# Masking the strided heads of four batches by a multiplication on VectorE, and spreading the first expert's weights

## The chip, the cores and the metric

The kernel runs on one core of one Trainium2 chip. The metric is the device time of one execution in microseconds. A core has five engines with queues of their own: TensorE (PE, with its weight loads shown apart as PEld), VectorE (DVE), ScalarE (ACT), GpSimd (POOL) and SyncE (SP, which here only issues transfers).

## The reference

Two blocks follow each other: sparse attention, then a mixture of experts with one expert for each token.

```python
# attention: batch 8, heads 8, S = 576, head size 64
rel = pos[:, None] - pos[None, :]
mask_local = (rel >= 0) & (rel < 32)
mask_strided = (rel >= 0) & (pos[None, :] % 32 == pos[:, None] % 32)
masks = mask_local for heads 0 to 3, mask_strided for heads 4 to 7
scores = np.where(masks, q @ k.T / np.sqrt(D), -1e9)
attn = softmax(scores);  x = attn @ v          # heads side by side: 576 x 512 for each batch
# experts: 8 experts, 512 -> 1024 -> 512
logits = x @ w_gate;  local_gate = sigmoid(x @ w_local)
e = argmax(logits) if s == 0 or local_gate < 0.5 else the previous token's e
out = p[e] * (relu(x @ w1[e]) @ w2[e])         # p: softmax of the logits
```

A masked score contributes nothing to the numerator and nothing to the sum. Setting it far below zero ahead of the exponential, or multiplying its exponential by zero, gives the same sum.

## The kernel before

The kernel has two stages: attention with the router (function `attention`, up to about 165 us), then the experts (`Experts.run`, to the end). The change is in the first.

**Steps.** Attention runs over 32 pairs of heads, batch by batch: pairs 0 and 1 of a batch are local, 2 and 3 strided. Each pair is two units (`Unit`, g = 0 and 1). The loop at L433 is software-pipelined by hand (the scheduler is off, so each engine's queue has the order of the program text). Step n issues, in this order: the load of q and k of pair n + 4 (L436); a piece of the first expert's weights in steps 5 to 12 (L438); scores and mask of the two units of pair n (L442, L443); the store of x of a pair finished two steps ago (L445); the transposes of pair n - 2 (`turn_x`, L447); values and norm of pair n - 1 (L450, L451); up to two of the weights' sums (L457); for finished batches the gates (L463), the store of probabilities and the logits (L467); and router work of the list `also` (L472). So step 4b + 2 carries the gates of batch b - 1, and step 4b + 1 its logits.

**A strided pair.** The 576 positions are split into 32 residue classes of 18. Four blocks hold 7 classes (126 positions) and one holds 4 (72). Within a block, two positions of different classes must not see each other. Unit 0 covers two blocks, unit 1 two and the small one. `scores` makes the score block keys by queries with the two heads on separate halves of TensorE's rows (L261), ScalarE takes the exponential out of PSUM (L265), `values` multiplies by v with a column of ones (L285), and `norm` divides by the sum on VectorE (reciprocal L298, product L299).

**The masks before.** A local unit's exponentials are multiplied by 0 or 1 on VectorE (L272). A strided unit gets its mask ahead of the scores: TensorE multiplies an identity in bf16 by `maskS` (0 or -8e9) into the PSUM bank, two matmuls for each unit (L255), and the scores accumulate on top.

**Logits and gates.** `logits` (L348) multiplies the transposed x by the router's weights into the one bank of `psT`; ScalarE and VectorE copy it out in turn (L351, L352, L354, L357), and the exponentials of the next step stand behind these copies in ScalarE's queue. `turn_x` uses the same bank. `gates` (L367 on TensorE, then twelve small operations L372 to L392 on VectorE and one on ScalarE) takes a buffer of `psV`, which has two: it must wait until `norm` has read it.

**The first expert's weights.** `Weights.load` brings them in eight pieces of 512 KB through SP's queue (w1 in four, L706, then w2 in four, L709). The experts multiply matrices of two by two blocks with seven products in place of eight, for which sums of weight blocks are needed: 16 operations of 128x512 on VectorE (`Weights.sums`, L714), made from step 10 on, two in a step. Router work of the first four batches begins at step 19: transposes of the codes (19), a scan (L547, step 20), counts (L550 to L554, step 21), slots (22), their way back (23), and a table from 24 on (`where` L609 to L614, `what` L620, `some` L627).

**Loads.** Buffers for q and k are five (`inp`), so a load waits on SP until a step's scores are done. From batch 2 on SP also issues the stores of x (L311, L317; twelve for each batch).

Of the kernel before, what the change touches and what calls it, by code (L numbers as in the profile page):

```python
# [8 lines left out]
F32 = mybir.dt.float32  # L9
# [3 lines left out]
Alu = mybir.AluOpType  # L13
# [6 lines left out]
B, H, S, DH = 8, 8, 576, 64  # L20
# [19 lines left out]
GK, GL = PL * GC, PL * GR  # L40
# [18 lines left out]
WARM = 10  # L59

FILL = 4

ARMS = 7
SKIP = 8192
# [18 lines left out]
def across(ap, shape):  # L83

    return ap.rearrange("a (o b) -> a o b", o=1).to_broadcast(shape)
# [60 lines left out]
def attention(ctx, tc, qkl, qks, vl, vs, wg, xd, ident, router, moe):  # L146

    nc = tc.nc
    sums, probs, codes = router.sums, router.probs, router.codes
    consts = ctx.enter_context(tc.tile_pool(name="consts", bufs=1))  # L150
# [28 lines left out]
    def busy(n):  # L179
        for _ in range(n):  # L180
            ps = psV.tile([P, 512], F32, name="vps")
            nc.tensor.matmul(ps, lhsT=warm[:, 0:P], rhs=warm, start=True, stop=True)  # L182
# [23 lines left out]
    maskS = consts.tile([GK, 2 * GK + GL], BF16, name="maskS")  # L206
# [3 lines left out]
    for n, c in blocks:  # L210

        i, div = consts.tile([GK, 1], I32, name=f"row{n}"), consts.tile([GK, 1], F32, name=f"div{n}")
# [7 lines left out]
    n = GK  # L220
    nc.vector.tensor_copy(maskS[:, 0:2 * n].rearrange("p (a x) -> p a x", a=2), across(apart[n], [n, 2, n]))
    nc.vector.tensor_copy(maskS[:, 2 * n:], apart[GL])
    fold = consts.tile([P, E + 1], F32, name="fold")
    ci = consts.tile([P, E], I32, name="ci")
    down = consts.tile([P, E], F32, name="down")
    pi = consts.tile([P, CH], I32, name="pi")
    pos8 = consts.tile([P, CH], F32, name="pos8")
    start = consts.tile([P, CH], F32, name="start")

    def more_constants():  # L230

        nc.vector.tensor_reduce(fold, ident.rearrange("p (k x) -> p x k", k=DK)[:, 0:E + 1], axis=AX.X, op=Alu.add)


        nc.gpsimd.iota(ci, pattern=[[-1, E]], base=E, channel_multiplier=0)
        nc.vector.tensor_copy(down, ci)
        nc.gpsimd.iota(pi, pattern=[[E * P, CH]], base=E, channel_multiplier=E)
        nc.vector.tensor_copy(pos8, pi)
        nc.vector.tensor_scalar(start, pos8, float(E), None, Alu.is_equal)

    def spans(u):

        if u.local:
            return [(3 * u.g + i, LQ, i * LQ) for i in range(3)]
        return [(j, GK if j < GT - 1 else GL, i * GK) for i, j in enumerate(range(2 * u.g, 2 + 3 * u.g))]

    def scores(u):
        t = st["qk", u.b, u.pair]
        kb, width = (LK, LQ) if u.local else (GK, GK)
        ps = psS.tile([P, 2, 512], F32, name="sps")  # L250
        sp = spans(u)
        n = sp[-1][2] + sp[-1][1]
        if not u.local:
            for h in range(2):
                nc.tensor.matmul(ps[0:GK, h, 0:n], lhsT=identb[0:GK, 0:GK],  # L255
                                 rhs=maskS[:, 0:n], start=True, stop=False, skip_group_check=True)
        for j, w, c in sp:
            m = kb if u.local else w
            for h in range(2):
                r = slice(h * DH, (h + 1) * DH)  # L260
                nc.tensor.matmul(ps[0:m, h, c:c + w], lhsT=t[r, S + j * width:S + j * width + m],  # L261
                                 rhs=t[r, j * width:j * width + w],
                                 start=(u.local and c == 0), stop=True, skip_group_check=True)
        e = work.tile([P, 2, 2 * GK + GL], F32, name="e")
        nc.scalar.activation(e[0:kb, :, 0:n], ps[0:kb, :, 0:n], Act.Exp, bias=0.0, scale=1.0 / DH ** 0.5)  # L265
        u.e = e

    def mask(u):
        if u.local:
            ev = u.e[:, :, 0:3 * LQ]  # L270
            m = maskL[:, 3 * u.g:3 * u.g + 3].rearrange("p a x -> p (a x)")
            nc.vector.tensor_tensor(ev, ev, m.rearrange("p (o x) -> p o x", o=1).to_broadcast([LK, 2, 3 * LQ]),  # L272
                                    op=Alu.mult)

    def values(u):
# [26 lines left out]
    def store_x(u):  # L302

        q = nc.gpsimd if u.b < 2 else nc.sync
        src = st["x", u.b, u.local]
        dst = xd[u.b * S:(u.b + 1) * S, (0 if u.local else D // 2):(D // 2 if u.local else D)]
        for a in range(2):
            if u.local:
                w = LQ // 2
                o = dst.rearrange("(t a p) d -> a p t d", a=2, p=w)[a]  # L310
                q.dma_start(out=o, in_=src[a * (P - w):a * (P - w) + w])  # L311
                continue
            for j in range(GT):
                c = GC if j < GT - 1 else GR
                w = c * PL // 2
                o = dst.rearrange("(p c) d -> p c d", c=STRIDE)[a * PL // 2:(a + 1) * PL // 2, j * GC:j * GC + c]
                q.dma_start(out=o, in_=src[a * (P - w):a * (P - w) + w, j])  # L317

    def turn_x(b, pair):
        if pair == 0:  # L320
            st["xT", b] = rows.tile([P, DK, S], F32, name="xT")
        local = pair < PAIRS // 2
        src = st["x", b, local][:, :, (pair % 2) * P:(pair % 2 + 1) * P]
        ps = psT.tile([P, 8, P], F32, name="tps")
        n = LT if local else GT
        for t in range(n):
            nc.tensor.transpose(ps[:, t], src[:, t], ident)  # L327
        o = st["xT", b][:, pair]

        def halves(o, i, w):  # L330
            nc.scalar.copy(out=o.rearrange("p (t a x) -> p t a x", a=2, x=w // 2),
                           in_=pick_halves(i, w))

        if local:
            halves(o, ps[:, 0:LT], LQ)
        else:
            halves(o[:, 0:4 * GK], ps[:, 0:GT - 1], GK)
            halves(o[:, 4 * GK:], ps[:, GT - 1:GT], GL)
# [55 lines left out]
    def store_p(b):  # L394
        dst = xd[b * S:(b + 1) * S, D:DX]
        full = S // P
        nc.gpsimd.dma_start(out=dst[0:full * P].rearrange("(t p) c -> p t c", p=P), in_=probs[:, 0:full, b])
        nc.gpsimd.dma_start(out=dst[full * P:], in_=probs[0:S - full * P, full, b])
# [14 lines left out]
        u.n = n  # L413

    also = {n: [] for n in range(len(units) + 3)}
    also[1] = [more_constants]
    also[2] = [router.constants]
    n = PAIRS * RB + 3
# [4 lines left out]
    m = n  # L423
    rooms = (moe.spot[0].rearrange("p a x -> p (a x)")[:, 0:1024], moe.spot[1].rearrange("p a k x -> p (a k x)"),
             moe.spot[2].rearrange("p i a x -> p (i a x)"))
    early = router.table(0, bank, rooms)
# [5 lines left out]
    steps = []  # L432
    for n in range(len(units) + 3):  # L433
        if n < len(units):
            if n + ahead < len(order):
                load(*order[n + ahead])  # L436
            if 5 <= n < 13:
                moe.W[0].load(nc, moe.w1, moe.w2, 0, n - 5)  # L438
            if n == 10:
                steps = moe.W[0].sums(nc.vector)  # L440
            for u in units[n]:
                scores(u)  # L442
                mask(u)  # L443
        if 0 <= n - 2 < len(units) and order[n - 2][1] % 2 == 1:
            store_x(units[n - 2][1])  # L445
        if 0 <= n - 2 < len(units) and n != len(units):
            turn_x(*order[n - 2])  # L447
        if 0 <= n - 1 < len(units):
            for u in units[n - 1]:
                values(u)  # L450
                norm(u)  # L451
        if n == len(units):
            turn_x(*order[n - 2])
            moe.turn(moe.first, spare, 0)
        elif n == len(units) + 1:
            busy(FILL)
        for do in steps[:2]:  # L457
            do()
            steps.remove(do)
        for b in range(B):  # L460
            last = PAIRS * b + PAIRS - 1
            if n == last + 3:
                gates(b)  # L463
            if n == last + 4 and b < B - 1:
                store_p(b)
            if n == last + 2:
                logits(b)  # L467
        if n == len(units) + 1:
            moe.turn(moe.first, bank, 1)
            busy(2)  # L470
            moe.row_sums(moe.first)
        for do in also[n]:  # L472
            do()
# [1056 lines left out]
```

## Time and profile before

| | us |
|---|---|
| median of three runs | 689.92 (687.54 to 690.97) |
| the profiled execution, whole | 686.27 |
| its span, first to last instruction | 684.5 |
| TensorE busy in the span | 666.4 |
| VectorE busy in the span | 356.7 |
| ScalarE busy in the span | 198.2 |
| mask matmuls L255, 64 of them, first and last start | 10.4 and 153.2 |
| multiplications L272, 32 of them, mean of one | 0.753 |

Durations below are from the one profiled execution. In lines of the timeline the columns are start, duration, engine, line, operation, output and input with shapes, count, and in brackets the idle time of the engine before and what ended it. In the chain of waits they are start, duration, engine, output tile and line. A TensorE matmul's end is modelled and neighbours overlap, so the chain's pieces, not the mean durations, say what a group of matmuls takes. Most fp32 matmuls appear as two records.

### The profile page before, as it was taken

How to read it: one execution, taken by the hardware profiler on the slowest of the kernel's cores; microseconds unless marked ns; L12 is line 12 of the kernel's file. 1: busy time of each engine (PE TensorE's matmuls, PEld its weight loads, DVE VectorE, ACT ScalarE, POOL GpSimd, SP SyncE). 2: the span in 40 equal slices, each digit the busy share in tenths (PEclk: the TensorE clock that was granted, in tenths of full speed). 3: DMA queues.
4: the chain of work that ended last, by engine and by line, in shares of the span. 5: the costliest groups of instructions: out<-in, count | busy, mean ns of one | idle time of the engine just before them, and what ended most of it. 6: DMA issues, size and time to landing. Idle time of an engine off the chain costs nothing.

```text
span 684.5 us, 14864 instructions
## 1 busy us (share of the span) xinstructions
PE 666.4 (97%) x6055; PEld 574.2 (84%) x6056; DVE 356.7 (52%) x821; ACT 198.2 (29%) x365; POOL 117.7 (17%) x144
## 2 busy tenths in 40 slices
PE   9999999999999999999999999999999999999994
PEld 6888887887998999589989999997799899699493
DVE  6558866865895437126532654651256546522131
ACT  3454453544312221222222122122222132221220
POOL 3440000012021113111111202202111113121001
PEclk9999999999999999999999999999999999999998
DMA  9999878733611172171236118111612622021001
GB/s 322 402 377 329 274 250 279 255 114 121 226 36 43 50 268 76 40 275 40 57 120 204 56 29 294 51 32 40 251 48 65 234 75 72 34 57 41 18 9 35
DMA packets 35800, 95.80 MB, mean 140 GB/s; under 512 B 4790, under 2 KB 11702, under 8 KB 35628
## 3 DMA queue, kind: packets, MB, share of 16 engines
q1 hardware_dynamic: 27164, 71.41, 29.6%
q0 software_dynamic: 7936, 22.38, 10.1%
q8 instruction: 66, 1.08, 0.6%
q14 instruction: 106, 0.87, 0.4%
q10 hardware_dynamic: 528, 0.07, 0.1%
HBM read 74.66 MB, written 19.69 MB: 138 GB/s over the span
## 4 chain that ended last, share of the span: by engine, by line
PE 93%; DVE 3%; issue 1%; ACT 1%; DMA 1%; POOL 0%; SPq 0%; DVEq 0%; POOLq 0%
PE lps L817 30%; PE mps L853 28%; PE sps L261 6%; PE vps L285 5%; PE lps L908 4%; PE mps L919 4%; PE tps L327 3%; PE xps L760 2%; PE mps L949 2%; PE lps L929 2%; PE sps L255 2%; PE vps L367 1%; PE tps L348 1%; DVE xl L299 1%; PE vps L182 1%
## 5 line engine op out<-in xcount | busy, mean ns | idle before, releaser
L773 POOL DMA_INDIRECT out_dram<-y,tab x40 | 46.1, 1153 | 351.4 <-DVE y L805 247.4
L817 PE MATMUL lps<-tt,ws 128*128 128x128 f32 x768 | 91.8, 275 | 0.3 <-issue 0.3
L817 PEld LDWEIGHTS lps<-tt,ws 128*128 128x128 f32 x768 | 88.6, 192 | 0.6 <-issue 0.5
L853 PE MATMUL mps<-wt,k 128*128 128x256 f32 x384 | 85.7, 380 | 0.0
L853 PEld LDWEIGHTS mps<-wt,k 128*128 128x128 f32 x384 | 72.8, 190 | 9.9
L817 PE MATMUL lps<-xt,w1t 128*128 128x128 f32 x512 | 63.2, 276 | 3.0 <-ACT y L955 1.9
L817 PEld LDWEIGHTS lps<-xt,w1t 128*128 128x128 f32 x512 | 60.4, 192 | 6.5 <-ACT y L955 3.7
L805 DVE TENSOR_TENSOR h<-lps,u 128x512 f32<-128x512 f32 x48 | 33.2, 691 | 58.3 <-PE lps L817 58.2
L853 PE MATMUL mps<-w2t,h 128*128 128x256 f32 x256 | 60.5, 379 | 0.0
L747 POOL DMA_INDIRECT x<-xd,gi x40 | 41.1, 1027 | 84.8 <-issue 34.7
L265 ACT ACTIVATE e<-sps 128x576 f32<-128x576 f32 (+1 forms) x64 | 41.3, 650 | 40.0 <-PE sps L261 39.2
L853 PEld LDWEIGHTS mps<-w2t,h 128*128 128x128 f32 x256 | 47.4, 190 | 5.8
L261 PE MATMUL sps<-qk 64*128 64x96 f32 (+2 forms) x704 | 51.2, 283 | 0.1
L804 ACT ACTIVATE h<-h 128x512 f32<-128x512 f32 x48 | 30.3, 630 | 70.1 <-DVE h L805 69.0
L261 PEld LDWEIGHTS sps<-qk 64*128 64x128 f32 (+2 forms) x704 | 43.1, 185 | 8.5 <-issue 7.2
L804 ACT ACTIVATE h<-lps 128x512 f32<-128x512 f32 (+1 forms) x28 | 15.7, 563 | 81.8 <-PE lps L817 65.6
L805 DVE TENSOR_TENSOR u<-lps,p 128x512 f32<-128x512 f32 x16 | 11.1, 691 | 52.5 <-PE lps L817 31.6
L753 ACT ACTIVATE x<-x 128x512 f32<-128x512 f32 (+1 forms) x40 | 27.1, 717 | 34.5 <-DMA x<-xd,gi 21.1
L761 ACT COPY xt<-xps 128x512 f32<-128x512 f32 (+1 forms) x38 | 20.3, 565 | 49.3 <-PE xps L760 49.3
L817 PE MATMUL lps<-xt,ws 128*128 128x128 f32 x256 | 31.3, 275 | 0.0
L817 PE MATMUL lps<-tt,w1t 128*128 128x128 f32 x256 | 31.3, 275 | 0.0
L853 PE MATMUL mps<-w2t,k 128*128 128x256 f32 x128 | 30.4, 380 | 0.0
(236 smaller groups left out, 974.5 us busy)
## 6 DMA issues: line engine op xcount, KB each, us to landing
w1t<-in_w_dram SPq DMA_DIRECT2D x7, 2048.0 KB
w2t<-in_w_dram SPq DMA_DIRECT2D x7, 2048.0 KB
qk<-in_qkl_dram SPq DMA_DIRECT2D x16, 592.0 KB
qk<-in_qks_dram SPq DMA_DIRECT2D x16, 576.0 KB
vl<-in_vf_dram SPq DMA_DIRECT2D x8, 780.0 KB
vs<-in_vg_dram SPq DMA_DIRECT2D x8, 639.8 KB
xd<-xl SPq DMA_DIRECT2D x12, 288.0 KB
xd<-xs SPq DMA_DIRECT2D x48, 63.0 KB
```

Source lines behind the costliest of these rows:

```text
L261: nc.tensor.matmul(ps[0:m, h, c:c + w], lhsT=t[r, S + j * width:S + j * width + m], rhs=t[r, j * width:j * width + w], start=(u.local and ...
L265: nc.scalar.activation(e[0:kb, :, 0:n], ps[0:kb, :, 0:n], Act.Exp, bias=0.0, scale=1.0 / DH ** 0.5)
L285: nc.tensor.matmul(ps[a * HALF:(a + 1) * HALF, h, i], lhsT=u.e[0:m, h, q0:q0 + HALF], rhs=vt[0:m, j, 2 * i2 + h], start=(i == 0 and h == 0 ...
L747: self.nc.gpsimd.indirect_dma_start(out=r.x[0:r.m, i], out_offset=None, in_=self.xd[0:r.rows], in_offset=bass.IndirectOffsetOnAxis(ap=r.gi ...
L753: self.nc.scalar.activation(r.x[0:r.m, i, 0:D], r.x[0:r.m, i, 0:D], Act.Copy, scale=r.gate[i][0:r.m])
L773: s = self.nc.gpsimd.indirect_dma_start(out=self.out, out_offset=bass.IndirectOffsetOnAxis(ap=r.si[i][0:r.m], axis=0), in_=y[0:r.m, i], in ...
L804: relu = lambda o, i: nc.scalar.activation(o, i, Act.Relu)
L805: add = lambda o, i, p: nc.vector.tensor_tensor(o, p, i, op=Alu.add)
L817: nc.tensor.matmul(ps[:, f], lhsT=m[:, kk, f * P:(f + 1) * P], rhs=v[:, kk], start=(start and f == 0 and kk == 0), stop=(kk == 1), skip_gr ...
L853: nc.tensor.matmul(ps[:, 0:256], lhsT=m[:, f], rhs=v[:, f], start=(start and f == 0), stop=(f == 3), skip_group_check=True)
L908: nc.tensor.matmul(ps[:, f], lhsT=w.w1[:, kk, c:c + P], rhs=r.xt[:, 0, kk], start=(f == 0 and kk == 0), stop=(kk == DK - 1), skip_group_ch ...
L919: nc.tensor.matmul(ps, lhsT=h[f // 4][:, f % 4], rhs=w.w2[:, f], start=(f == 0), stop=(f == FK - 1))
```

## The change

The strided units of the first four batches (`MB = 4`) no longer get the two mask matmuls. Their exponentials are multiplied on VectorE by `near`, a tile of 0 and 1 made once, in step 0, from `maskS`. For this the strided arrays in DRAM hold k ahead of q, so that the last block's weights may be read as 126 columns wide (54 of them belong to q, and their rows of scores are not used); all rows of the PSUM block are then written. The strided units of batches 4 to 7 keep the mask matmuls.

The eight pieces of the first expert's weights are loaded in steps 5, 7, ..., 19 in place of 5 to 12. Their 16 sums begin at step 13 in place of 10; one is made in each of the steps 13 to 20, two in each of 21 to 24.

```diff
+MB = 4
...
+    near = consts.tile([GK, 2 * GK + GL], F32, name="near")
...
+    def masks():
+        nc.vector.tensor_scalar(near, maskS, 0.0, None, Alu.is_equal)
...
-        if not u.local:
+        early = u.b < MB
+        if not u.local and not early:
             for h in range(2):
                 nc.tensor.matmul(ps[0:GK, h, 0:n], lhsT=identb[0:GK, 0:GK],
                                  rhs=maskS[:, 0:n], start=True, stop=False, skip_group_check=True)
         for j, w, c in sp:
-            m = kb if u.local else w
+            m = kb if u.local or early else w
...
+                k0, q0 = (S, 0) if u.local else (0, S)
...
+        elif u.b < MB:
+            n = 2 * GK + (GL if u.g else 0)
+            ev = u.e[0:GK, :, 0:n]
+            nc.vector.tensor_tensor(ev, ev, near[:, 0:n].rearrange("p (o x) -> p o x", o=1).to_broadcast([GK, 2, n]),
                                     op=Alu.mult)
...
+    also[0] = [masks]
...
-            if 5 <= n < 13:
-                moe.W[0].load(nc, moe.w1, moe.w2, 0, n - 5)
-            if n == 10:
+            if 5 <= n < 21 and n % 2:
+                moe.W[0].load(nc, moe.w1, moe.w2, 0, n // 2 - 2)
+            if n == 13:
                 steps = moe.W[0].sums(nc.vector)
...
-        for do in steps[:2]:
+        for do in steps[:1 if n < 21 else 2]:
...
-    qks = np.concatenate([heads(classes(i["q"][:, h2:])), heads(classes(i["k"][:, h2:]))], 3)
+    qks = np.concatenate([heads(classes(i["k"][:, h2:])), heads(classes(i["q"][:, h2:]))], 3)
```

More of the change, by code (lines that the diff above doesn't have):

```diff
@@ L257, in scores @@
         for j, w, c in sp:
-            m = kb if u.local else w
+            m = kb if u.local or early else w
             for h in range(2):
                 r = slice(h * DH, (h + 1) * DH)
-                nc.tensor.matmul(ps[0:m, h, c:c + w], lhsT=t[r, S + j * width:S + j * width + m],
-                                 rhs=t[r, j * width:j * width + w],
-                                 start=(u.local and c == 0), stop=True, skip_group_check=True)
+                k0, q0 = (S, 0) if u.local else (0, S)
+                nc.tensor.matmul(ps[0:m, h, c:c + w], lhsT=t[r, k0 + j * width:k0 + j * width + m],
+                                 rhs=t[r, q0 + j * width:q0 + j * width + w],
+                                 start=((u.local or early) and c == 0), stop=True, skip_group_check=True)
         e = work.tile([P, 2, 2 * GK + GL], F32, name="e")
@@ L272, in mask @@
             nc.vector.tensor_tensor(ev, ev, m.rearrange("p (o x) -> p o x", o=1).to_broadcast([LK, 2, 3 * LQ]),
+                                    op=Alu.mult)
+        elif u.b < MB:
+            n = 2 * GK + (GL if u.g else 0)
+            ev = u.e[0:GK, :, 0:n]
+            nc.vector.tensor_tensor(ev, ev, near[:, 0:n].rearrange("p (o x) -> p o x", o=1).to_broadcast([GK, 2, n]),
                                     op=Alu.mult)
```

## The prediction

> **What bounds the kernel now.** I read the page first, then who waited for whom on TensorE, then the chain of waits, then the timeline of single steps. A step n is one pair of heads (batch n // 4, pair n % 4).
>
> ```profile
> span 684.5 us, 14864 instructions
> PE 666.4 (97%) x6055; PEld 574.2 (84%) x6056; DVE 356.7 (52%) x821; ACT 198.2 (29%) x365; POOL 117.7 (17%) x144
> DMA  9999878733611172171236118111612622021001
> PE vps L367 <- DVE sums L298: 2.3, 7, 0.6
> ```
>
> TensorE is the bound: it idles 18 us in all. The change lies in the attention stage, up to 165 us, where the largest TensorE wait (last line: 2.3 us, 7 times) is the gate matmuls L367 waiting until VectorE has normalised the step before. DMA is full for some 65 us, yet no TensorE wait names a load.
>
> ```profile
> 27.70 0.36 PE sps L255 x2
> 28.06 0.64 PE sps L261 x8
> 28.70 0.42 PE sps L255 x2
> 29.12 0.76 PE sps L261 x12
> 38.07 1.51 PE sps L261 x24
> ```
>
> These pieces of the chain price a step's scores: strided 2.18 us (mask matmuls included), local 1.51 us, or 0.063 us for each of 24 records.
>
> ```profile
> 28.63 0.61 ACT L354 COPY lT<-tps 64x504 f32<-64x504 f32 x1 [0.29 <-DVE lT L352]
> 31.58 0.20 DVE L298 RECIPROCAL sums<-vps 128x6 f32<-128x6 f32 x1 [2.07 <-PE vps L285]
> 32.52 1.25 PE L367 MATMUL vps<-fold,lT 128*128 128x9 f32 x12 [0.28 <-DVE sums L298]
> 35.83 0.20 DVE L392 TENSOR_TENSOR probs<-ex,gsm 128x40 f32<-128x40 f32 x1
> 39.51 0.77 PE L327 MATMUL tps<-ident,xs 128*128 128x128 f32 x5
> 87.00 0.85 PE L327 MATMUL tps<-ident,xl 128*128 128x128 f32 x6 [0.34 <-DVE lT L357]
> 107.04 1.35 DVE L554 TENSOR_TENSOR_SCAN cum<-run 32x576 f32<-32x576 f32 x1
> ```
>
> These timeline lines are the joints used below: steps 6 to 8 (28 to 40 us), the end of the weights' sums (87 us), the router's scan (107 us). VectorE has 2.07 us of room in step 6, but at 87 and 107 us TensorE already waits behind it.
>
> ```profile
> L272 DVE TENSOR_TENSOR e<-e,maskL 128x576 f32<-128x576 f32 x32 | 22.8, 753 | 8.4 <-ACT e L265 8.4
> L714 DVE TENSOR_TENSOR ws<-w1t 128x512 f32<-128x512 f32 x16 | 10.5, 682 | 0.0
> ```
>
> The groups by shape price the added multiplication (as L272) and a weights' sum (0.68 us).
>
> [...] at 107 us norm waits behind a scan. [...] The trace shows 0.17 and 0.23 us of weight-load idling behind each pair of L255.
>
> **The change, part by part.**
>
> *Mask matmuls removed*, 8 strided steps (2, 3, 6, 7, 10, 11, 14, 15), 32 matmuls. What stays is 20 records, which at the local 0.063 take 1.26 us (the last block now loads 126 weight columns instead of 72, so I price it as a whole block). Each step is relieved by 2.18 - 1.26 = 0.92 us, 7.4 us in all, if nothing else is late.
>
> *Multiplications added*: two per strided step, 0.68 + 0.83 us, 12.1 us of VectorE in all. They stand ahead of norm(n-1) in VectorE's queue, and behind norm stand psV's release, the gate matmuls and turn_x. So another thing is late next:
>
> - Steps 6, 10, 14 (with gates). Exponentials wait for the logits' copies, not for the scores: L354 ends at 29.24, and two exponentials take 1.19 us where the scores are ready (67.41 us in the timeline), so they end at 30.46. The second multiplication ends at 31.32, and the reciprocal overlaps its end by 0.07: 31.25 against 31.58. Of 0.92 us only 0.33 arrives at L367.
> - Steps 7, 11, 15. The gates' small operations stand ahead of the multiplications and end (L392) at 36.03 - 0.33 = 35.70. Two multiplications back to back end at 37.08, norm takes 1.36 more (38.36), turn_x can start at 38.45. Before it started at 39.51. Together the two steps gain 1.06 (TensorE alone would give 1.25). Three batches: 3.2 us.
> - Steps 2, 3 (no gates). turn_x(0) waits for norm(0), at 12.0 instead of 12.59: 0.6. Then the router's constants (2.4 us of small operations) stand ahead of the multiplications of step 3, these end at 18.95, norm(2) at 20.25, turn_x(2) starts at 20.35 instead of 20.75. Of 1.84 us 0.4 is left.
>
> The new mask near (one tensor_scalar over 324) is not in the trace; between 0.2 us (a small cast) and 0.5 us, I take 0.4. It delays mask(1) by 0.1 us, and is in the 0.6 above; if its cover went, 0.4 us.
>
> *Weight loads* move from steps 5 to 12 (one each) to the odd steps 5 to 19. Each is 0.43 us of SP's queue and 512 KB, about 1.3 us at the 400 GB/s of the full stretches. From step 13 on a piece stands ahead of ten stores of x, which take 11 to 12 us on SP, and ahead of the next loads of q and k: at 73.68 us the load for step 18 is issued, used at 84.42. Some 1.7 us of those 10.7 go; I cost it at nothing. The early full stretch loses 2 MB, but no TensorE wait names it, so that gains nothing either.
>
> *Sums*: before two in each of steps 10 to 17; after one in 13 to 20, two in 21 to 24.
> - Gone: waits for lT (0.34 us at 87.00, some 0.08 at 67.80), since one sum fits before L352: 0.4 us. Single sums behind the multiplications of steps 14 to 17 end before the gates' first operation (33.36 against 33.48 in the times of step 6), so cost nothing.
> - New: in step 20 a sum goes ahead of the scan (100.07), which pushes mask(21) and norm(20) by 0.65. Two more sums then stand ahead of L352: they end at 106.05, and L352 starts at 105.98 instead of 104.85, 1.13 us late. L357 releases the bank that turn_x(20) needs, then come the count and norm(21), whose gate matmuls already wait: 1.1 us, all on the path.
> - Step 22: sums ahead of the gates' operations, 0.5 us, which reaches turn_x(21) through the one psT bank. Here the clock fell to 0.5 to 0.7 (111 to 115 us), which hid it; between 0 and 0.5, I take 0.2.
> - Step 23: 0.85 on L580, behind 1.05 of idle time: nothing.
> - Step 24: two sums ahead of the table's where (1.37), then mask(25), norm(24) and L352, 128.32 instead of 126.95; turn_x(24) starts at 129.55 instead of 128.36: 1.2 us.
> Together 2.5 us lost, bounds 1.5 and 3.2.
>
> Everything behind 165 us is a dense TensorE chain that moves along. Sum: -3.2 - 0.4 - 0.4 + 2.5 = -1.5 us. Against the profiled execution (686.27 us, span 684.5 and 1.8 around it) that is 684.8. The median of the runs shown is 3.65 above that execution, so I put the forecast at 689.92 - 1.5 = 688.4. About 0.5% (3.4 us) is what a measurement of this kernel can tell from no change; this is 0.2%.
>
> **Rivals.**
>
> *TensorE's relief arrives whole*: VectorE absorbs the multiplications. Then -7.4 - 0.4 + 2.5 = -5.3: 684.6; with the late sums hidden too, 682.1. For it: VectorE is 52% busy, and has 2 us of room in front of norm in several steps. Against: the second multiplication of step 6 cannot start before its exponential ends (30.46), 1.12 us before the reciprocal, and takes 0.83 of them; in step 7 the gates' operations fill the room. Chance 0.20.
>
> *VectorE becomes the bound in steps 20 to 26*: scan, count and table cannot move, and the nine sums there lie wholly on the path, 9 x 0.68 = 6.2 us, against gains of 4.0: +2.2, 692.1, slower than before. If step 3's pattern (other work ahead of the multiplications) also halves the batches' 3.2, 693.7. For it: TensorE waits behind the count already (0.58 us), and between 120 and 125 us (the table by stretches) VectorE is busy for 4.83 of 5 us. Against: ahead of the masks of steps 20 and 24 and the norm of step 23 it idles 1.33, 1.05 and 1.79 us. It decides from the point at which these 4.2 us are used up. Chance 0.16.
>
> *Loads come late*: SP's queue loses its 10 us lead in steps 13 to 22. A missed load costs a few microseconds a batch; two batches give 692 or more. Against: DMA falls to 0.34 at 70 to 75 us, so the backlog is gone by then. Chance 0.04.
>
> **How the numbers follow.** Forecast 0.60, rivals 0.20, 0.16, 0.04. The forecast's own range is from its bounds: gains between 2.7 and 5, losses 1.5 to 3.2, 686.4 to 690.4. The range on record takes in the first rival's 684.6 and the second's 692.1. Over 0.5% faster: the first rival and a small tail of the forecast, 0.22; slower by that much: half of the second, part of the third and the spread of medians, 0.12; within: 0.66.
>
> **What would show it.** Right: in the profile after, L367 of steps 6, 10 and 14 still waits for VectorE (0.5 us or more instead of 0.28); turn_x of step 8 starts behind the second norm, and the stretch from the logits of step 5 to those of step 9 is about 1.06 us shorter; near 105 and 127 us turn_x waits for lT by about a microsecond.  Wrong: if those stretches are 1.8 us shorter (first rival), if steps 20 to 26 take over 4 us longer than before (second), or if TensorE waits for qk (third).

## The result and the profile after

The changed kernel takes 688.41 us (median of 22 runs, 685.73 to 691.80), beside 690.68 us (22 runs) of the kernel before on the same chip: ratio 0.9985, 95% interval 0.9966 to 1.0003. (The ratio goes with the means of the executions, 688.75 and 689.79 us; the medians lie 2.3 us apart.) On the 689.92 us of before that is 1.0 us less, between 2.3 less and 0.2 more: no difference that can be told from nothing. The forecast of 688.4 us was right in the time, but so would a forecast of no change have been; what the change does has to be read from the traces. There its parts were not all right: both the gains and the loss were larger than I had put them.

Line numbers of the profiles from here on are those of the changed program: scores L270 (L261 before), mask matmuls L262, local multiplication L281, the new multiplication L286, values L299, reciprocal L312, product L313, `turn_x` L341, logits L362, their copies L365, L366, L368 and L371, gates L381, sums L729.

The first lines of the page of the kernel after, to be read beside those of before:

```profile
span 687.5 us, 14818 instructions
PE 663.8 (97%) x6024; PEld 574.5 (84%) x6024; DVE 367.6 (53%) x838; ACT 198.2 (29%) x365; POOL 118.8 (17%) x144
```

TensorE has 31 records fewer and is busy for 2.6 us less; VectorE has 17 more and is busy for 10.9 us more, near the 12.1 + 0.4 us that were added. TensorE's busy time fell by less than the 7.4 us of the forecast's full relief, since matmuls at half clock count as busy and take longer: the 12 records of L270 that score the second unit take 1.45 us in step 23, at a clock of 0.50, and 0.83 us in step 22, at 1.00 (between 6 us and the experts the profile after has 13.7 us of half clock, the one of before 3.4). And TensorE is idle for 23.7 us of the span, where it was 18.1. The view of who waits for whom, TensorE alone (us in total, times, longest):

```profile
PE tps L341 <- DVE lT L371: 3.9, 5, 1.0
PE vps L381 <- DVE sums L312: 2.2, 6, 0.8
PE vps L381 <- PE vps L299: 1.5, 1, 1.5
PE sps L270 <- DMA qk<-in_qks_dram: 0.5, 1, 0.5
```

The first line is new in this size: `turn_x` waits five times for the last copy of the logits (into the tile lT) out of the one bank of `psT`. The gates' wait, which I had expected to grow, stayed at 2.2 us.

**Where the time went, step by step.** The trace gives the start of the scores of each step; the difference to the profiled execution of before (positive: the kernel after is earlier):

| at the start of step | 2 | 6 | 7 | 8 | 12 | 16 | 18 | 19 | 22 | 24 | 26 | 27 | 30 | 31 |
|---|---|---|---|---|---|---|---|---|---|---|---|---|---|---|
| us earlier | 0.16 | 1.23 | 1.42 | 2.34 | 3.30 | 4.17 | 4.24 | 4.61 | 4.62 | 2.13 | 2.11 | 1.09 | 1.09 | -0.46 |

So 4.5 us are gained up to step 22, 3.5 are given back in steps 22, 23 and 26, and 1.6 more go in step 30. The experts behind take 519.4 and 519.5 us.

From step 6 to the start of step 8 of the kernel after, from the timeline (start, duration, engine, line, operation; in brackets the idle time before and what ended it):

```profile
27.41 0.61 ACT L368 COPY lT<-tps 64x504 f32<-64x504 f32 x1 [0.29 <-DVE lT L366]
28.04 1.19 ACT L274 ACTIVATE e<-sps 126x504 f32<-126x504 f32 x2
28.05 0.23 DVE L371 COPY lT<-tps 64x72 f32<-64x72 f32 x1 [0.67 <-ACT lT L368]
28.43 0.85 PE L341 MATMUL tps<-ident,xl 128*128 128x128 f32 x6 [0.70 <-DVE lT L371]
28.66 1.43 DVE L286 TENSOR_TENSOR e<-e,near 126x504 f32<-126x504 f32 x2 [0.38 <-ACT e L274]
30.17 0.20 DVE L312 RECIPROCAL sums<-vps 128x6 f32<-128x6 f32 x1
31.10 1.25 PE L381 MATMUL vps<-fold,lT 128*128 128x9 f32 x12 [0.28 <-DVE sums L312]
32.28 1.32 PE L270 MATMUL sps<-qk 64*126 64x126 f32 x20
34.53 1.42 DVE L286 TENSOR_TENSOR e<-e,near 126x504 f32<-126x504 f32 x2
37.17 0.77 PE L341 MATMUL tps<-ident,xs 128*128 128x128 f32 x5
```

In step 6 the scores are done 0.92 us sooner, and `turn_x` spends 0.70 of it on waiting for L371 (28.43): before, the mask matmuls had filled that time. Only 0.2 of the relief arrives. In step 7, and at the `turn_x` of step 8 (37.17), no bracket shows a wait, and the whole 0.92 arrives. The same `turn_x` of steps 6, 22 and 26 before, none of which waited:

```profile
29.81 0.87 PE L327 MATMUL tps<-ident,xl 128*128 128x128 f32 x6
106.35 0.88 PE L327 MATMUL tps<-ident,xl 128*128 128x128 f32 x6
128.36 0.87 PE L327 MATMUL tps<-ident,xl 128*128 128x128 f32 x6
```

In step 2, the first strided step, a load took part of the relief: the fourth line of the waits is the start of step 3 (14.43 us), to which TensorE comes 0.5 us before its q and k have landed.

The groups by shape up to 165 us, which price what was added (busy us, mean ns):

```profile
L286 DVE TENSOR_TENSOR e<-e,near 126x648 f32<-126x648 f32 x8 | 6.6, 827 | 0.0
L286 DVE TENSOR_TENSOR e<-e,near 126x504 f32<-126x504 f32 x8 | 5.4, 676 | 1.1 <-ACT e L274 1.1
L234 DVE TENSOR_SCALAR near<-maskS 126x324 f32<-126x324 bf16 x1 | 0.3, 323 | 0.0
```

The two means, 676 and 827 ns, agree with the 0.68 and 0.83 us of the forecast, which were an estimate. A straight line through the two means of before, 682 ns at 512 elements and 753 at 576, gives 0.67 and 0.83 us, as an estimate too. Steps 22 and 26, TensorE in the timeline:

```profile
102.48 0.85 PE L341 MATMUL tps<-ident,xl 128*128 128x128 f32 x6 [0.74 <-DVE lT L371]
105.70 1.25 PE L381 MATMUL vps<-fold,lT 128*128 128x9 f32 x12 [0.82 <-DVE sums L312]
127.30 0.85 PE L341 MATMUL tps<-ident,xl 128*128 128x128 f32 x6 [0.99 <-DVE lT L371]
```

These are the forecast's late waits, at the places it named. What comes around the gates of step 22 is in the table by stretches (length; busy time and count of PE, PEld, DVE, ACT and POOL; granted clock, DMA share, GB/s):

```profile
104.00:107.00 3.00, 2.18 (x47) 2.02 (x42) 2.90 (x7) 0.01 (x1) 0.00 (x0) 1.00 0.78 278
108.00:111.00 3.00, 3.00 (x24) 2.21 (x21) 2.59 (x13) 0.82 (x3) 1.14 (x2) 0.50 0.48 94
111.00:114.00 3.00, 3.00 (x40) 2.67 (x41) 0.45 (x2) 1.18 (x2) 0.18 (x1) 0.50 0.99 329
```

From 107.4 to 114.3 us the clock is at 0.50, in the profile of before only from 111.4 to 114.8, and in a second profile of before not at all. The table for 111 to 115 us in these two:

```profile
111.00:115.00 4.00, 4.00 (x29) 3.11 (x28) 2.88 (x16) 1.54 (x3) 1.32 (x2) 0.57 0.77 249
```

```profile
111.00:115.00 4.00, 3.84 (x53) 2.97 (x54) 3.20 (x17) 1.85 (x4) 1.22 (x2) 1.00 0.66 218
```

So step 23 takes 5.77 us at full clock (second profile of before), 7.06 with one stretch of half clock (first profile) and 8.58 with two, and with the sums ahead of it (after). In step 30, the longest single stall of VectorE:

```profile
150.18 0.20 DVE L312 RECIPROCAL sums<-vps 128x6 f32<-128x6 f32 x1 [2.73 <-PE vps L299]
```

The matmuls that it waits for are done by about 148.8. The gates then wait 1.5 us (the third line of the waits), and the clock is halved from 151.8 to 158.6. The kernel before has this stall too, as its second profile shows below.

### The profile page after: what moved, and what is told of

It reads as the page before. It is cut to its first block, busy times and chain, and to the rows that moved or that the text cites. A ratio compares the mean times of both kernels' runs of the same rounds, so it can differ in the third digit from the quotient of the medians.

```text
span 687.5 us, 14818 instructions
## 1 busy us (share of the span) xinstructions
PE 663.8 (97%) x6024; PEld 574.5 (84%) x6024; DVE 367.6 (53%) x838; ACT 198.2 (29%) x365; POOL 118.8 (17%) x144
## 4 chain that ended last, share of the span: by engine, by line
PE 90%; DVE 4%; DMA 2%; ACT 1%; issue 1%; SPq 0%; POOL 0%; DVEq 0%; POOLq 0%; ACTq 0%
PE lps L832 30%; PE mps L868 28%; PE vps L299 5%; PE sps L270 5%; PE lps L923 4%; PE mps L934 4%; PE tps L341 3%; PE xps L775 2%; PE mps L964 2%; PE lps L944 2%; DMA qk<-in_qks_dram 2%; PE vps L381 1%; PE tps L362 1%; DVE xl L313 1%; PE sps L262 1%
## 5 line engine op out<-in xcount | busy, mean ns | idle before, releaser
L270 PE MATMUL sps<-qk 64*128 64x96 f32 (+3 forms) x704 | 50.5, 286 | 0.6 <-DMA qk<-in_qks_dram 0.5
L270 PEld LDWEIGHTS sps<-qk 64*128 64x128 f32 (+2 forms) x704 | 43.8, 192 | 6.4 <-issue 3.9
```

The source lines that it names most:

```text
L270: nc.tensor.matmul(ps[0:m, h, c:c + w], lhsT=t[r, k0 + j * width:k0 + j * width + m], rhs=t[r, q0 + j * width:q0 + j * width + w], start=( ...
```

## The experiments

Edits are shown against the changed kernel. "Step 18 is 2.1 us earlier" always means the start of its scores beside the first profile of before.

### The multiplication alone

```diff
-            if 5 <= n < 21 and n % 2:
-                moe.W[0].load(nc, moe.w1, moe.w2, 0, n // 2 - 2)
-            if n == 13:
+            if 5 <= n < 13:
+                moe.W[0].load(nc, moe.w1, moe.w2, 0, n - 5)
+            if n == 10:
...
-        for do in steps[:1 if n < 21 else 2]:
+        for do in steps[:2]:
```

> The multiplication stays, the weights' loads (steps 5 to 12) and sums (two in each of steps 10 to 17) are those of before. Theory A (the multiplication gains, the sums in steps 20 to 24 give back 2 us): the scores of step 10 start 2.3 us earlier than before, those of step 18 some 3.5 earlier (two sums a step now delay the gates of step 14), and nothing is given back in steps 20 to 26, so step 30 still stands 3 us or more earlier; about 686.5 to 687.5 us against 690.5. Rival (the multiplication only fits because the sums were thinned out): with two sums in a step VectorE is full in steps 10 to 17, step 18 starts less than 1.5 us earlier, and the whole is not faster than before.

Measured: 687.69 us (14 runs), ratio 0.9993 (0.9967 to 1.0020). Step 12 is 3.31 us earlier, as in the kernel after, but step 13 only 2.28 and step 18 only 2.06. The timeline shows where it went:

```profile
50.75 0.69 DVE L729 TENSOR_TENSOR ws<-w1t 128x512 f32<-128x512 f32 x1 [0.71 <-DMA w1t<-in_w_dram]
55.60 0.41 PE L341 MATMUL tps<-ident,xs 128*128 128x128 f32 x2 [0.58 <-DVE sums L312]
66.25 0.85 PE L341 MATMUL tps<-ident,xl 128*128 128x128 f32 x6 [1.18 <-DVE lT L371]
85.48 0.85 PE L341 MATMUL tps<-ident,xl 128*128 128x128 f32 x6 [0.88 <-DVE lT L371]
```

The largest loss is that of step 12. A sum of step 10 waits 0.71 us for its weights to land (50.75). The gates' operations and the multiplications of step 11 stand behind it and come 1.3 us later than in the kernel after (53.48 against 52.16), and `turn_x` of step 12 waits for the norm behind those. Then, with two sums in each step, the copies L366 and L371 are later still: `turn_x` waits 1.18 us in step 14, where it was 0.75 in the kernel after, and 0.88 in step 18, where it was nothing. Nothing is lost in steps 22 to 26 (0.82 at 22 and at 27). My expectation for step 18, 3.5 us, was too high: I had not seen that the old pace of the sums and the multiplications get in each other's way, nor that an early sum can wait for its load.

### The spread alone

```diff
-MB = 4
+MB = 0
...
-    also[0] = [masks]
```

> The mask matmuls stay in all batches; only the weights' loads and sums are spread. Theory A: nothing is gained up to step 14, 0.4 us from the waits for lT in steps 14 and 18, and 2.2 us are lost in steps 20 to 26, so the scores of step 30 start 1.8 us later than before; about 1.0025 of before. Rival (the thinner loads relieve the full DMA queues): the steps up to 14 get shorter and step 30 starts no later than before.

Measured: 690.51 us (22 runs), ratio 1.0023 (1.0006 to 1.0040). Up to step 12 the difference is constant at 0.14 us, so loading later relieves nothing. Step 19 is 1.03 earlier: about half of that are the waits for lT in steps 14 and 18, which are gone, and 0.34 comes in step 13, where the scores took 1.91 us before and take 1.58 here, without a wait that explains it. Then the sums cost, TensorE in the timeline:

```profile
106.28 0.88 PE L341 MATMUL tps<-ident,xl 128*128 128x128 f32 x6 [0.96 <-DVE lT L371]
113.45 0.88 PE L341 MATMUL tps<-ident,xl 128*128 128x128 f32 x6 [0.52 <-DVE total L576]
```

0.98 us from step 22 to 23 and 1.03 from 26 to 27. From 23 to 24 it gains 0.93, because the first profile of before has a stretch of half clock there and this one has not; against the second, which has none either, it loses 0.35 (6.12 us against 5.77). So without any half clock the sums cost 2.4 us. By their ratios the two halves alone give about 0.5 us less (2.3 less to 1.4 more) and 1.6 us more (0.4 to 2.8), where both together give 1.0 less; these intervals are too wide to say that the halves don't add up. The traces say it: at step 19 the halves are 1.52 and 1.03 us earlier, both together 4.61. Sums that begin later and come one at a time make room for the multiplications.

### The sums kept out of steps 20 to 27

```diff
-        for do in steps[:1 if n < 21 else 2]:
+        for do in steps[:{19: 2, 23: 1, 28: 1, 29: 1, 30: 1, 31: 2, 32: 2}.get(n, int(n < 19))]:
```

> As the changed kernel, but the sums of steps 20 to 24 stand in steps where VectorE idled: one in each of 13 to 18, two in 19, one in 23, 28, 29 and 30, two in 31 and 32. Theory A (the sums beside the router's scan and table are on the path): the waits for lT in steps 22 and 26 (0.74 and 0.99 us) go, step 30 starts about 4 us earlier than before instead of 1.1, the whole is 2 to 3 us faster than the changed kernel, about 0.994 to 0.9955 of before. Rival (what was lost in steps 22 to 24 is the half clock of TensorE that falls there anyway): step 30 starts less than 2.5 us earlier than before.

One sum stays in step 23, none in the other seven of these steps. Measured: 684.70 us (9 runs), ratio 0.9927 (0.9899 to 0.9954). Step 22 is 4.91 us earlier, step 26 4.90, step 28 4.90: of the loss nothing is left, though one stretch of half clock stands at 107.0 to 110.4, as in the first profile of before. TensorE's wait for the copies, which was 3.9 us in five places, is now

```profile
PE tps L341 <- DVE lT L371: 2.2, 3, 0.8
```

and the three are steps 6, 10 and 14. Repeated on another chip, with the expectation

> The late sums once more, on the same chip as the two runs above. It should be 0.9925 to 0.995 of the kernel before, as in its first run, with step 22 starting 4.9 us earlier than in the first profile of the kernel before.

it took 682.64 us (7 runs), ratio 0.9956 (0.9936 to 0.9976). The ratio lies a little outside what was expected, and the two intervals overlap. That profile lost 0.8 us in step 4, where `turn_x` waited for norm, and 1.5 us between steps 19 and 20 to a half clock (88.4 to 91.8 us), so step 22 is only 2.72 earlier; in steps 22 to 28 it, too, gives nothing back.

### turn_x behind the values

```diff
+        first = n in (6, 10, 14)
-        if 0 <= n - 2 < len(units) and n != len(units):
+        if 0 <= n - 2 < len(units) and n != len(units) and not first:
...
+        if first:
+            turn_x(*order[n - 2])
```

> As the changed kernel, but in steps 6, 10 and 14 the transposes turn_x(n - 2) come behind values(n - 1), so that TensorE has work while the psT bank is still held. Theory B (in these steps the psT bank is what is late, 0.7 us of waiting): the wait goes and each of the three steps is 0.5 to 0.7 us shorter, step 18 starts about 2 us earlier than in the changed kernel. Theory C (the multiplications, which end just before the reciprocal, are equally late): the transposes no longer wait, but L381 waits 0.7 to 0.8 us instead of 0.28, and the steps are as long as in the changed kernel within 0.1 us.

Measured: 690.69 us (22 runs), ratio 1.0020 (1.0003 to 1.0036). Step 6 gains 0.22 and step 7 0.93, as in the kernel after (0.19 and 0.92). The wait has only moved, in the timeline of TensorE to the gates:

```profile
49.80 1.25 PE L381 MATMUL vps<-fold,lT 128*128 128x9 f32 x12 [0.98 <-DVE sums L312]
69.02 1.25 PE L381 MATMUL vps<-fold,lT 128*128 128x9 f32 x12 [1.04 <-DVE sums L312]
```

0.98 is 0.70 + 0.28. So what limits step 6 is not the order on TensorE. By the trace it is the copies: `turn_x` waits for the last one, and the exponentials, the multiplications and norm stand behind them; no run moves the copies themselves. This kernel's profile is later at step 18 (0.93 us earlier than before, the kernel after 4.24) mostly because of what followed the waits, in the table by stretches:

```profile
48.00:51.00 3.00, 2.02 (x22) 1.77 (x20) 2.25 (x6) 0.64 (x1) 0.57 (x1) 1.00 1.00 382
51.00:55.00 4.00, 4.00 (x41) 3.54 (x41) 3.40 (x14) 1.84 (x4) 1.38 (x2) 0.57 1.03 298
```

A stretch of half clock stands at 51.2 to 54.6 us and another at 71.7 to 75.1. Step 11 takes 1.4 us longer than in the kernel after, step 15 1.5. The mean clocks of the 22 executions, 0.982 to 0.991, against 0.985 to 0.994 of the kernel after, fit that.

### Every multiplication twice

```diff
-            nc.vector.tensor_tensor(ev, ev, near[:, 0:n].rearrange("p (o x) -> p o x", o=1).to_broadcast([GK, 2, n]),
-                                    op=Alu.mult)
+            for _ in range(2):
+                nc.vector.tensor_tensor(ev, ev, near[:, 0:n].rearrange("p (o x) -> p o x", o=1).to_broadcast([GK, 2, n]),
+                                        op=Alu.mult)
```

> As the changed kernel, but each multiplication of the first four batches' strided units is made twice (the mask is 0 or 1, so the second changes nothing): 12 us more on VectorE. Theory C (the multiplications end just before the reciprocal of steps 6, 10 and 14, and norm of steps 7, 11 and 15 has little room): steps 6, 10 and 14 become 1.4 us longer each, steps 7, 11 and 15 some 0.5 to 0.8 longer, step 18 starts 5 to 6 us later than in the changed kernel, that is 1 to 2 us later than before. Rival (VectorE, 53% busy, still has room for them): step 18 starts less than 2 us later than in the changed kernel.

Measured: 699.23 us (4 runs), ratio 1.0168 (1.0098 to 1.0237). Step 18 is 13.6 us later than in the kernel after, for 12 us of added VectorE time; I had expected 5 to 6. Lines of TensorE's timeline (the line numbers from the multiplication on are one higher here):

```profile
22.88 0.41 PE L342 MATMUL tps<-ident,xs 128*128 128x128 f32 x2 [2.54 <-DVE sums L313]
37.81 1.25 PE L382 MATMUL vps<-fold,lT 128*128 128x9 f32 x12 [1.81 <-DVE sums L313]
58.55 1.25 PE L382 MATMUL vps<-fold,lT 128*128 128x9 f32 x12 [1.81 <-DVE sums L313]
```

In steps 6, 10 and 14 the waits are what I expected, norm behind the multiplications: the gates of steps 6 and 10 wait 1.53 us more than in the kernel after, for 1.5 us added. In steps 7, 11 and 15, where I had expected 0.5 to 0.8 us, TensorE waits for nothing. These steps are 1.4 to 1.6 us longer all the same, because a stretch of half clock falls into each (at 40.5, 60.9 and 81.4 us, behind the gates' wait), as one does into step 4 (at 23.4). Together the four cost about 6 us, so about 7.5 of the 13.6 are waits. The half clock also hides a wait: norm's first product, which `turn_x` of step 8 needs, ends at 44.79 us, and `turn_x` starts at 45.44; by an estimate from these figures, TensorE would have come to it 1.5 us sooner at full clock, ahead of the product. The single multiplication is thus just hidden, with little to spare in steps 7, 11 and 15 and nothing in 6, 10 and 14.

### Before, once more

> The kernel before once more, for a second profile. Theory D (the stall of VectorE in step 30, near 150 us, and the half clock behind it are there in the kernel before too, and its first profile is one of the executions without): this profile shows VectorE's reciprocal of step 30 one to three microseconds late, clock near 0.5 for some us behind it, and a span near 687 to 689. Rival (the stall belongs to the changed kernels, all five of which show it): the reciprocal follows its matmuls as in the first profile, span near 684.5.

A second profile of the unchanged kernel took 687.97 us, span 686.1. Of its timeline, step 30 (the first is a GpSimd gather for the experts):

```profile
148.55 1.05 POOL L747 DMA_INDIRECT x<-xd,gi  x1 [13.03 <-PE tps L327]
150.93 0.20 DVE L298 RECIPROCAL sums<-vps 128x6 f32<-128x6 f32 x1 [3.06 <-PE vps L285]
151.86 1.25 PE L367 MATMUL vps<-fold,lT 128*128 128x9 f32 x12 [1.93 <-remote]
```

The stall of step 30 is in the kernel before too, and a stretch of half clock (154.3 to 157.7) behind it; there is none at 111 to 115 this time. Its experts start at 167.4 us, the first profile's at 165.0, those of after at 168.1. So the first profile of before was an execution without this stall, and the 1.6 us in step 30 need not be a cost of the change: the second profile loses as much there.

### The gather a step later

```diff
-    also[m + 5].append(lambda: moe.gather(moe.first))
+    also[m + 6].append(lambda: moe.gather(moe.first))
```

on top of the sums kept out of steps 20 to 27.

> As e3 (late sums), but GpSimd's gather of the first expert's rows is issued at the end of step 30 in place of 29; it leaves nothing out. Theory E (VectorE's stall of step 30 is tied to the gather on GpSimd): the stall leaves step 30 and appears, if at all, in step 31. Rival (it is tied to that place in VectorE's own instruction stream): it stays in step 30. The time is not expected to be better than e3's: the scaled rows come later.

Measured: 685.33 us (17 runs), ratio 0.9944 (0.9925 to 0.9964). The edit missed its aim: the two gathers still ran at 145.3 and 146.6 us, and the stall stayed (2.79 us idle ahead of the reciprocal). Whether the gather makes the stall is not settled by it. In the profiles without the stall (the first of before and those of the last three runs below) the gather stands at the same place, 3.2 us behind the start of step 30, so its presence alone is not enough. As a repeat of the sums kept out of steps 20 to 27 the run counts.

### The multiplication in all eight batches

```diff
-MB = 4
+MB = 8
```

again with the sums kept out.

> As e3, with the multiplication in all eight batches. If the gain of a batch (1.1 us) were general, 4 more batches would bring 4.4 us, about 680 us. Theory C says that VectorE's order decides: in batches 5 and 6 (steps 22, 23, 26, 27) scan, count and table already stand ahead of norm, so these steps gain nothing or lose; at most 2 us, and the whole between 1 us slower and 2 us faster than e3.

Measured: 699.57 us (4 runs), ratio 1.0160 (1.0108 to 1.0212), 14 us above the late sums on the same chip (685.33, the run before this), where I had expected at most 1. Step 20 is 5.10 us earlier, with 1.05 from batch 4; step 24 is 2.34 earlier, step 26 0.50 later and step 30 2.72 later. TensorE in the timeline, steps 22 to 26:

```profile
105.63 1.25 PE L381 MATMUL vps<-fold,lT 128*128 128x9 f32 x12 [2.14 <-DVE sums L312]
109.43 1.54 PE L341 MATMUL tps<-ident,xl 128*128 128x128 f32 x6 [0.91 <-DVE total L577]
132.83 1.25 PE L381 MATMUL vps<-fold,lT 128*128 128x9 f32 x12 [1.68 <-DVE sums L312]
```

From step 20 on scan, count, slots and table fill VectorE, and the multiplications go straight on the path; stretches of half clock (108.0 to 121.7, 135.3 to 138.7 us) follow.

### The multiplication in five batches

```diff
-MB = 4
+MB = 5
```

again with the sums kept out, on the chip of its repeat above.

> The late sums, with the multiplication in the first five batches. Theory (TensorE is the bound through step 19 as long as the sums are sparse): batch 4 gains what batches 1 to 3 gained, 1.06 us over its steps 18 and 19, so the start of step 20 is 1.0 to 1.2 us earlier than in the run of the late sums, and the time is some 1 us below it, about 0.9985 of it. Rival (the multiplications of step 18 and 19 meet the sums there): the gates of step 18 wait 0.5 us or more, as in steps 20 on in the run with all eight batches, and the gain is nil.

Measured: 680.81 us (7 runs), ratio 0.9926 (0.9900 to 0.9952); the repeat on the same chip took 682.64. Steps 18 and 19 together take 9.87 us, in the first run of the late sums 10.92: 1.05 from batch 4. The timeline of TensorE in step 18:

```profile
83.57 0.84 PE L341 MATMUL tps<-ident,xl 128*128 128x128 f32 x6 [0.45 <-DVE lT L371]
86.25 1.25 PE L381 MATMUL vps<-fold,lT 128*128 128x9 f32 x12 [0.28 <-DVE sums L312]
```

The gates wait no longer than elsewhere, so the rival falls. Step 20 itself starts 4.36 us earlier, less than the 4.90 of the late sums' first profile and not more, because in this profile TensorE waited 1.87 us for the load of q and k of step 3, where the other waited 0.45. This version is 0.5 to 1.0% faster than the kernel before, and its profile is the shortest of the study; against the late sums alone the times (682.64 and 680.81) point the same way as the trace, but their intervals overlap.

### Two matmuls ahead of the gates of step 22

```diff
+                if n == 22:
+                    for _ in range(2):
+                        nc.tensor.matmul(spare()[:, 0:512], lhsT=warm[:, 0:P], rhs=warm, start=True, stop=True)
                 gates(b)
```

again on the late sums.

> The late sums, with two bf16 matmuls of 128x512 into a bank of the scores ahead of the gates of step 22; they compute nothing that is read. Theory F (the idle time of TensorE at the gates is what brings the half clock): the wait of 0.65 us of the gates of step 22 is filled, no half clock at 106 to 111 us, 1.7 us less in the steps behind 22 than in the profile of the late sums. Rival (the windows of half clock fall independent of so short a wait): one stands there all the same, and the time is the same or up to 0.3 us longer, by the two matmuls.

Measured: 683.60 us (22 runs), ratio 0.9970 (0.9957 to 0.9984). The gates' wait is filled, this profile has no half clock anywhere from 14 to 174 us, and step 23 takes 5.77 us where both profiles of the late sums, with one stretch in it, took 7.04 and 7.05. In the table by stretches, the same 4 us of this kernel, of the repeat of the late sums, and of the kernel with the later gather:

```profile
107.00:111.00 4.00, 3.84 (x43) 3.04 (x42) 2.91 (x18) 1.54 (x3) 0.71 (x1) 1.00 0.45 153
```

```profile
107.00:111.00 4.00, 4.00 (x38) 3.11 (x38) 2.91 (x18) 0.83 (x2) 0.57 (x1) 0.73 0.24 74
```

```profile
107.00:111.00 4.00, 3.83 (x44) 3.12 (x44) 2.91 (x18) 1.50 (x3) 0.55 (x1) 1.00 0.61 216
```

The second waited 0.64 us ahead of the gates and lost its clock, the third waited the same 0.64 and did not. And the time is not below that of the repeat (682.64). So the profile agrees with the theory, but the third had no half clock there without any filling, and the times don't support it: a wait of this length is not enough by itself, and filling it brought nothing that can be measured.

## Why the prediction was right or wrong

**Batches 1 to 3: right in the sum, wrong in its two halves.** Predicted 3.2 us, measured 1.11, 0.96 and 1.18, so 3.25. "Of 0.92 us only 0.33 arrives at L367" was 0.19, and step 7 gave 0.92, not 0.73. The forecast let the multiplications end step 6; `turn_x` is first in TensorE's queue and waited there for L371. I had used the end of the copies (L354) for the exponentials and not followed the next copy to the bank that `turn_x` needs. The experiment with `turn_x` behind the values shows that the multiplications are next in line anyway, some 0.1 us later than I had put them. In step 8 turn_x(6) came as early as predicted (37.17 in its own time, 38.40 in that of before; predicted 38.45), and TensorE reached it at that very moment, so that it shows no wait.

**The sign that I named was wrong.** The gates of steps 6, 10 and 14 wait 0.28 us as before, and not 0.5 or more: the 0.70 us were lost ahead of them, one instruction group earlier. The other signs held: steps 6 and 7 together are shorter by 1.11 us for 1.06, and `turn_x` waits about a microsecond (0.74 and 0.99) in steps 22 and 26.

**Batch 0: mis-sized.** Predicted 0.4, measured 1.1 (1.23 at step 6 less 0.16 at step 2). The load of step 3 took 0.50 us of step 2's relief, which the forecast does not have. Against that stands the step that failed, turn_x(2) "at 20.35". It started at 19.32, 1.43 ahead of before: the router's constants and the multiplications of step 3 ended 0.5 us sooner than I had put them, at 18.44, and `turn_x` starts on the first unit's product (18.57 to 18.99) and needs the second only for its last ones (the line at 22.88 in the experiment with doubled multiplications shows two of its five matmuls standing apart). I had let it wait for both.

**Waits for lT behind the sums: right.** 0.37 us from step 18 to 19; predicted 0.34 for that place.

**The late sums: right in place, and in size but for the clock.** Predicted 2.5 us: 1.1 in step 22, 0.2 for the clock and the bank behind its gates, 1.2 in step 26. In the kernel after, step 22 lost 0.98, step 23 1.52 and step 26 1.02. The idle time fits steps 22 and 26: 0.74 at `turn_x` and 0.24 more at the gates (0.82 against 0.58 in before), and 0.99 in step 26. The term that I had at 0.2 is what failed. I had treated the half clock as a cover that hides part of the loss; but two stretches of it fell into step 23, where the first profile of before has one, and most of the 1.52 is the second one. Without any half clock the spread alone loses 0.35 there and 2.4 in all, near the 2.5. That the second stretch comes from the sums is not shown: the kernel with `turn_x` behind the values has the same sums and the same two waits in step 22 (0.75 and 0.82), and no half clock behind them. The late sums experiment recovers the whole loss.

**The rivals.** The whole relief did not arrive in steps 6, 10 and 14, as said against the first. The second, VectorE as the bound in steps 20 to 26, has its place right and its size wrong: the nine sums cost 2.4 us, 3.5 with the clock, not the 6.2 put down (9 x 0.68 is 6.1). It becomes true when multiplications stand there as well (eight batches). Loads of q and k came late nowhere in steps 13 to 22, where the third had looked for them; the one late load is that of step 3, ahead of every moved piece, and TensorE waits 0.50 us for it in the kernel after. The few microseconds a batch that the third put on a missed load were an estimate.

**From sum to time.** 4.5 gained and 3.5 lost are 1.0, against 1.5 predicted and 1.0 measured by the ratio. That the first profile of before was a lucky one, so that the forecast had to be set on the median, is shown by its second profile; that this agrees so closely is partly luck. Single executions of the kernel after lie 6 us apart, the gains were half a microsecond larger than put and the loss a whole one, which cancel in part, and the base has one stretch of half clock in step 23 where the kernel after has two.

Left open: what stalls VectorE in step 30 in most profiles but not in all (2.7 to 3.9 us idle with, 1.4 to 1.5 without; it goes otherwise with eight batches). The three changed kernels without it ran on one chip, on which none of 29 executions of before was above 688.2 us, while 29 of 74 on the two other chips of the experiments were above 690. Whether the chip decides is not tested. Open as well are gaps of about 0.3 us on TensorE that the profile calls "issue".

## What to carry to other kernels

Work that is moved from the bound engine to one with room is worth what the queue of the other engine lets through in each step: follow every instruction that the freed engine meets next, its PSUM bank too, since the first one to wait takes the gain. Two changes that share an engine are not priced apart: here, at step 19, the halves were 1.5 and 1.0 us earlier and both together 4.6. The shortest times came from asking in which steps VectorE has room, with the multiplications up to the step where the router's scan begins and most of the sums outside the steps of the router. When one profiled execution is the base of a sum, profile the same kernel a second time before a microsecond is put down to a change.

## What the runs showed of the hardware

Half the clock came in stretches of 3.41 us or of two or four times that: 111.4 to 114.8 us in the first profile of before, 107.4 to 114.3 after, 108.0 to 121.7 with eight batches. In the clock records of the traces of before and after the stretches of full clock ahead of and between these are whole multiples of it as well (the last stretch of half clock, at the kernel's end, 8.59 and 8.72 us, is not one): 105.81 us (31 times) ahead of the one of before, 102.40 us (30 times) ahead of the first one of after, 37.55 us (11 times) between the two of after. In these two traces the clock thus changes only on a grid of 3.41 us. A stretch cost less than the 1.7 us that half of it would be: step 23 takes 5.77 us without (in three profiles), 7.04 to 7.06 with one (in five), 8.58 with two and the sums ahead of it; elsewhere one cost 1.4 to 1.6 us.

Outside step 30, the longest TensorE wait ahead of such a stretch was 2.5 us (each multiplication twice), and several stood behind a wait of 0.6 to 1.0 us at the gates (0.58 before, 0.82 after, 0.98 and 1.04 with `turn_x` behind the values). One stretch (88.4 to 91.8 us, the repeat of the late sums) followed a wait of only 0.28 us. On the other side, in step 22 waits of 0.58, 0.64, 0.65 and 0.82 us went without one in four profiles, and waits of 1.87, 1.96 and 2.03 us for the load of step 3 in three. So no length of wait could be named from which it comes.

It goes with much of the spread: of the 22 executions of the kernel after, those of 685.7 to 686.6 us have mean clocks of 0.990 to 0.994, those of 691.2 to 691.8 all 0.987; the lowest clock, 0.985, belongs to one of 689.3.
